# Reordering the front of a fused attention and SwiGLU block on one core: load order, rounding order, and where the attention units are placed

## The chip, the core and the metric

The kernel runs on one core of a Trainium2 chip. The metric is device time in microseconds (us) of one launch. The engines are named as in the profile: PE multiplies matrices, DVE works on vectors, ACT computes activations and copies, POOL (GpSimd) is a second vector engine that cannot read PSUM, and SP issues transfers. PE loads its weights ahead of its matmuls; this shows as PEld. Each engine works through its own queue in order and waits for the others by semaphores. Transfers issued by SP and ACT run on 16 shared DMA engines.

## The reference

The block takes 2048 rows of 448 numbers in float32. It normalises each row, computes attention of 16 heads of width 28 that share one key and one value projection, adds the result to the input, normalises again, and applies a SwiGLU block of width 1792 with a second residual.

```python
xn = layernorm(x)                       # no scale, no shift, eps 1e-5
q  = (xn @ wq) in 16 heads of 28;  k = xn @ wk;  v = xn @ wv   # wk, wv: 448 x 28
p  = softmax(q @ k.T * 28 ** -0.5)
h  = x + (p @ v, heads side by side) @ wo
y  = layernorm(h)
out = h + (silu(y @ w1) * (y @ w3)) @ w2
```

## The kernel before

The rows are cut into four quarters t of 512 (`X[t]`, four blocks n of 128 rows each). Products that need float32 precision are made of three matmuls with rounded operands (type float32r): an operand a is split into a rounded part and the remainder, and rounded times rounded, remainder times rounded, and rounded times remainder are summed in one PSUM bank. `mm_D` does this over the 448 inputs, which are three blocks of 128 and one of 64. The last block carries the rounded part in partitions 0 to 63 and the remainder in 64 to 127, so a full product is 3 x 3 + 2 = 11 matmuls. `mm_D` calls `between` after the sixth of them, so that other matmuls can stand inside a product.

The order of work is written out by hand (the pool is set to a manual schedule): each engine's queue has its instructions in the order in which the Python code makes them. There are eight PSUM banks; `bank()` hands out the one that was given back longest ago, and a matmul into it waits until the earlier user's readers are done.

**The front** is everything ahead of the main loop. It does the following.

- Loads. SP issues X[0] in four blocks, then WQ (line 408, three transfers), then X[1] to X[3] (line 410). ACT issues WK and WV (line 407, three transfers each: three full blocks, and the 64-row block twice). The transfers share eight semaphores, so a later transfer also waits until an earlier one on the same semaphore has landed.
- Weights. `split_wkv` (L429 to L431) copies WK to a second place and makes the rounded part of WK and WV on ACT and the remainder on POOL. `split_wq` (L441) rounds WQ in four steps on ACT; `low_wq` (L437) makes the four remainders on POOL.
- Layer norm of quarter t. `ln_stats` (L178, L179) on DVE; `ln_rstd` adds eps on DVE (L183) and takes the power -0.5 on POOL (L184); `ln_norm` (L189) subtracts the mean and multiplies by the inverse root on DVE, one block at a time, and a narrow copy on POOL (L191) repeats the last 64 columns. The loop calls it with `spare` for POOL.
- `tr(t)`: four times `ln_tr`. PE transposes four blocks (L203), ACT rounds the result into `xh` (L211), DVE takes the remainder into `xl` (L221; L223 for the last 64 columns). For t = 0 the transposes of the first column block are interleaved with `heat`, matmuls whose results are not used (L420).
- `kv(t)`: keys and values. ACT copies them out (L473, L475), SP copies the keys to partitions 64 to 127 (L476), and, for odd t, POOL subtracts the keys of the quarter before (L478, `KD`). `k_low(t)` takes the remainder of the keys on DVE (L483), SP copies it (L484), and the bank is given back. `va(t)` transposes the values (L490) and copies them (L491).
- `q(t, g)`: queries of four heads. ACT copies them out (L502); for the first it rounds them, and DVE takes the remainder (`build_qs`, L238, L239).
- `quads()`: the row maxima of the scores for the softmax, for two quarters of keys at a time. A unit is four heads by 128 queries by 512 keys. Its first half multiplies the queries with the key difference `KD`, and ACT takes the positive part (L257, L267); its second half multiplies with the keys of the first quarter, and DVE adds both and takes the maximum (L271). Each half takes four banks. The list `first` holds twenty halves in order, and one call of `quads()` issues the next one.

The part of the written order that the change touches stands in lines 516 to 563. The **main loop** then goes over 16 groups of four heads and 512 queries and 16 blocks of keys (lines 629 to 660): scores and exponentials (L308, L318), products with the values (L326), and the row maxima of the groups ahead (L257, L263). The feed-forward part follows (lines 749 to 773).

Of the kernel before, what the change touches and what calls it, by code (L numbers as in the profile page):

```python
# [8 lines left out]
F32 = mybir.dt.float32  # L9
F32R = mybir.dt.float32r  # L10
AF = mybir.ActivationFunctionType
ALU = mybir.AluOpType
# [4 lines left out]
P = 128  # L17
S = 2048
D = 448
H = 16  # L20
DH = 28
F = 1792
T = 512
NT = S // T
NQ = T // P
# [15 lines left out]
def block_kernel(  # L41
# [13 lines left out]
    ve, se, ge, pe, sy = nc.vector, nc.scalar, nc.gpsimd, nc.tensor, nc.sync  # L55
    xv = x[0].rearrange("(t p n) d -> t p n d", t=NT, p=P, n=NQ)
# [3 lines left out]
    def f(ap):  # L60
        return ap.bitcast(F32)
# [4 lines left out]
    ln_pool = ctx.enter_context(tc.tile_pool(name="ln", bufs=2))  # L66
# [5 lines left out]
    X = [keep.tile([P, NQ, D], F32, name=f"X{t}") for t in range(NT)]  # L72
    ident = keep.tile([P, P], F32, name="ident")
    NEG = [keep.tile([P, 32], F32R, name="neg")] * 2
    NGT = [keep.tile([P, 32], F32, name=f"ngt{k}") for k in range(2)]
    pexp = keep.tile([P, NQ], F32, name="pexp")
# [3 lines left out]
    def slot(k, dt, name):  # L80
        return slots.tile([P, 2, T], dt, name=name, tag=f"slot{k}")

    QSP, PTP, WSP, HIDP = [4, 0, 1], [9, 5, 6, 7, 8], [(0, 1), (2, 3), (4, 5)], [6, 7, 8, 9]
    KD = slot(2, F32R, "kd")
# [6 lines left out]
    KH = keep.tile([P, S], F32R, name="KH", tag="kh")  # L91
# [37 lines left out]
    def bank(name="pb"):  # L129
        k = free.pop(0)  # L130
        ps = ps_w.tile([P, T], F32, name=name, tag=f"bank{k}") if k < 7 else ps_o.tile([P, T], F32, name=name, tag="po")
        used[id(ps)] = ps, k
        return ps

    def done(ps):
        free.append(used.pop(id(ps))[1])
# [2 lines left out]

    def mm_D(ps, lhs, rhs, lsl, rsl, between=None, part=False):


        terms = []
        for a, b in ((0, 0), (1, 0), (0, 1)):
            terms += [(a, c, b, c) for c in range(3)]
        terms += [(0, 3, 0, 3), (0, 3, 1, 3)][: 2 - part]
        for k, (a, ca, b, cb) in enumerate(terms):
            pe.matmul(  # L150
                ps, lhs[b][:, cb, lsl], rhs[a][:, ca, rsl],
                start=(k == 0), stop=(k == len(terms) - 1 and not part),
            )
            if between is not None and k == 5:
                between()

    def load_w(dst, w, eng=sy):
        eng.dma_start(dst[:, 0:3], w[0:384].rearrange("(c p) m -> p c m", p=P))
        eng.dma_start(dst[0:64, 3], w[384:448])
        eng.dma_start(dst[64:128, 3], w[384:448])  # L160
# [9 lines left out]
    LN = {}  # L170

    def ln_stats(t, n):
        if n == 0:
            LN[t] = (ln_pool.tile([P, NQ, 6], F32, name="st", bufs=NT),
                     ln_pool.tile([P, NQ, 2], F32, name="mv", bufs=NT),
                     ln_pool.tile([P, NQ], F32, name="rs", bufs=NT), {})
        st, mv, _, _ = LN[t]
        ve.bn_stats(st[:, n], X[t][:, n])  # L178
        ve.bn_aggr(mv[:, n], st[:, n])  # L179

    def ln_rstd(t, n0=0, n1=NQ):
        _, mv, rs, _ = LN[t]
        ve.tensor_scalar(rs[:, n0:n1], mv[:, n0:n1, 1], EPS, None, op0=ALU.add)  # L183
        ge.tensor_tensor(rs[:, n0:n1], rs[:, n0:n1], pexp[:, n0:n1], op=ALU.pow)  # L184

    def ln_norm(t, n, spare=False):
        _, mv, rs, xns = LN[t]
        xn = xns[n] = ln_pool.tile([P, 512], F32, name="xn", bufs=4)
        (ge if spare else ve).tensor_scalar(xn[:, :D], X[t][:, n], mv[:, n, 0:1], rs[:, n : n + 1],  # L189
                                            op0=ALU.subtract, op1=ALU.mult)  # L190
        ge.tensor_copy(xn[:, D:], xn[:, 384:D])  # L191

    XT = {}
# [35 lines left out]
    def build_qs(i, ps=None, spare=False):  # L229
        t, g = divmod(i, NG)  # L230
        QS[i] = slot(QSP[i % 3], F32R, "qs")
        MX[i] = MXS[i % 2]
        qh, ql = QS[i][:, 0], QS[i][:, 1]
        q = QR[t][:, g] if ps is None else ps
        if spare:
            ge.tensor_copy(qh, q)
        else:
            se.activation(qh, q, AF.Copy)  # L238
        (ge if ps is None else ve).tensor_tensor(ql, q, f(qh), op=ALU.subtract)  # L239
# [159 lines left out]
    def wkv(tl, k):  # L399
        return tl[:, k, :384].rearrange("p (c m) -> p c m", c=4)  # L400

    RELU2, VT = slot(5, F32, "relu2"), slot(8, F32, "vt")
    wkv_r, WKV = wkv(slot(7, F32, "wkv"), 0), slot(6, F32R, "wkvs")
    WKV = [wkv(WKV, k) for k in range(2)]
    ve.memset(wkv_r, 0.0)
    for m0, w in ((0, wk), (64, wv)):
        load_w(wkv_r[:, :, m0 : m0 + DH], w, se)
    load_w(wq_r, wq)
    for t in range(1, NT):
        sy.dma_start(X[t], xv[t])  # L410
    kb = keep.tile([64, 1], F32, name="kb")
    ge.tensor_tensor(kb, ident[:64, 28:29], ident[:64, 60:61], op=ALU.add)
    for k in range(2):
        ve.memset(f(WQ[k][:, :, :, DH:]), 0.0)
    se.activation(NGT[0][:, :P // 4], ident[:, :P // 4], AF.Copy)
    warm = bank()

    def heat(n):
# [16 lines left out]
    def low_wq(c0, c1, eng):  # L435
        for c in range(c0, c1 + 1):
            eng.tensor_tensor(WQ[1][:, c, :, :DH], wq4[:, c], f(WQ[0][:, c, :, :DH]), op=ALU.subtract)  # L437

    def split_wq(c0, c1, eng=None):
        for c in range(c0, c1 + 1):  # L440
            se.activation(WQ[0][:, c, :, :DH], wq4[:, c], AF.Copy)  # L441
            if eng:
                low_wq(c, c, eng)

    def load_wo():
        ge.memset(wo_r, 0.0)
        wov = wo.rearrange("(g j r) e -> j r g e", j=4, r=DH)
        for j in range(4):
            sy.dma_start(wo_r[32 * j : 32 * j + DH], wov[j])
# [2 lines left out]
        ve.tensor_copy(WO[0][:, g], wo_r[:, g])  # L452
        ge.tensor_tensor(WO[1][:, g], wo_r[:, g], f(WO[0][:, g]), op=ALU.subtract)

    def stats(t, *ns):
        for n in ns:
            ln_stats(t, n)
        if NQ - 1 in ns:
            ln_rstd(t)

    def norm(t):
        for n in range(NQ):
            ln_norm(t, n)

    def tr(t, *cs):
        for c in cs or range(4):
            ln_tr(t, c)

    def kv(t, between=None):
        cols = slice(t * T, (t + 1) * T)  # L470
        ps = bank()
        mm_D(ps[:96], WKV, XT[t], slice(0, 96), slice(0, T), between)
        se.activation(KH[0:64, cols], ps[0:64], AF.Identity, bias=kb)  # L473
        vt = VT[:, t % 2]
        se.activation(vt[64:96], ps[64:96], AF.Copy)  # L475
        sy.dma_start(f(KH[64:128, cols]), f(KH[0:64, cols]))  # L476
        if t % 2:
            ge.tensor_tensor(KD[:, t // 2], f(KH[:, cols]), f(KH[:, (t - 1) * T : t * T]), op=ALU.subtract)  # L478
        return vt, ps

    def k_low(t, ps):
        cols = slice(t * T, (t + 1) * T)
        ve.scalar_tensor_tensor(KL[0:64, cols], ps[0:64], kb, f(KH[0:64, cols]), op0=ALU.add, op1=ALU.subtract)  # L483
        sy.dma_start(f(KL[64:128, cols]), f(KL[0:64, cols]))  # L484
        done(ps)

    def va(t, vt):
        ps = bank()
        for n in range(NQ):
            pe.transpose(ps[:, 32 * n : 32 * n + 32], vt[64:96, n * P : (n + 1) * P], ident[64:96, 64:96])  # L490
        ve.tensor_copy(VA[:, NQ * t : NQ * t + NQ, :DH],  # L491
                       ps[:, :P].rearrange("p (n r) -> p n r", n=NQ)[:, :, :DH])
        done(ps)

    def q(t, g, between=None):
        ps = bank()
        mm_D(ps, [w[:, :, 4 * g : 4 * g + 4].rearrange("p c h r -> p c (h r)") for w in WQ],
             XT[t], slice(0, P), slice(0, T), between)
        if t == g == 0:
            build_qs(0, ps)  # L500
        else:
            se.activation(QR[t][:, g], ps, AF.Copy)  # L502
        done(ps)
# [6 lines left out]
    def quads(n=1):  # L510
        while n > 0 and first:
            fn, *args = first.pop(0)
            fn(*args)
            n -= fn is quad

    for n in range(NQ):
        ln_stats(0, n)
        ln_rstd(0, n, n + 1)
        if n > 0:
            ln_norm(0, n - 1)  # L520
    ln_norm(0, NQ - 1)
    split_wkv()
    split_wq(0, 3)
    ln_tr(0, 0, between=lambda: heat(8))
    done(warm)
    tr(0, 1, 2, 3)
    low_wq(0, 3, ge)
    v0, p0 = kv(0)
    stats(1, 0, 1, 2, 3)
    q(0, 0)  # L530
    k_low(0, p0)
    norm(1)
    q(0, 1)
    tr(1)
    v1, p1 = kv(1)
    stats(2, 0, 1, 2, 3)
    q(0, 2)
    k_low(1, p1)
    norm(2)
    q(0, 3)  # L540
    va(0, v0)
    va(1, v1)
    build_qs(1)
    quads()
    tr(2)
    quads()
    v2, p2 = kv(2, quads)
    stats(3, 0, 1, 2, 3)
    q(1, 0, quads)
    k_low(2, p2)  # L550
    norm(3)
    quads()
    q(1, 1, quads)
    va(2, v2)
    quads()
    q(1, 2, quads)
    q(1, 3)
    build_qs(2)
    quads()
    tr(3)  # L560
    quads()
    v3, p3 = kv(3)
    load_wo()
    q(2, 0)
    k_low(3, p3)
# [14 lines left out]
    def at(s, fn, *args):  # L580
        todo.setdefault(s, []).append((fn, args))
# [8 lines left out]
    LAST = NC * NI  # L590
# [9 lines left out]
            at(e + 14 + 2 * n, ln_stats, t, n)  # L600
        at(e + 22, ln_rstd, t)
    for n in range(NQ):
        at(LAST - 24 + n, ln_norm, 0, n, True)
    for c in range(4):
        at(LAST - 17.5 + 4 * c, lambda c: ln_tr(0, c, True, True), c)
    for t in range(NT):
# [195 lines left out]
```

## Time and profile before

| | |
|---|---|
| median of three runs | 1195.46 us (1195.0 to 1196.61) |
| profiled execution, its own time | 1196.01 us |
| its span, first to last instruction | 1194.2 us |
| mean granted PE clock | 0.998 |
| PE busy | 1178.6 us, 99% |
| DVE, ACT, POOL busy | 811.2, 724.0, 332.4 us |
| first matmuls of the main loop | 92.75 us after the span's start |

The profile is read by rows. In an answer in order of time a row is: start, length in us, engine, line, operation, what is written and read, shapes, how many instructions were merged, and, in brackets, the idle time before and what ended it. `PEq`, `ACTq`, `SPq` are an engine's queue: issuing of a transfer, or waiting. A matmul's length includes its way through the array; successive matmuls start closer together than that. In a row of a group, the numbers behind the bar are the total busy time in us, the mean length of one in ns, and the idle time ahead of them with what ended it.

### The profile page before, as it was taken

What the parts mean: (1) busy time and instruction counts of PE and PEld (TensorE: products, weight loads), DVE (VectorE), ACT (ScalarE), POOL (GpSimd) and SP (SyncE); (2) the same over time, 40 slices, a digit from 0 to 9 for tenths busy, and PEclk for the clock granted to TensorE, in tenths of its full rate; (3) what the DMA queues carried; (4) which work ended last, traced back from release to release, by engine and by line L of the source; (5) the groups of instructions that cost most, each with busy time, mean ns of one, the idle gap of its engine ahead of it and who ended that gap; (6) DMA issues with size and microseconds to landing.
All of it is one profiled execution on the core that took longest, in us unless ns stands there. A gap on an engine that the chain in (4) does not pass through costs nothing. (4 is left out here: it accounts for less than half of the span.)

```text
span 1194.2 us, 24111 instructions
## 1 busy us (share of the span) xinstructions
PE 1178.6 (99%) x9594; PEld 728.6 (61%) x9594; DVE 811.2 (68%) x1486; ACT 724.0 (61%) x1377; POOL 332.4 (28%) x256
## 2 busy tenths in 40 slices
PE   8999999999999999999999999999999999999998
PEld 6664444445544445444445443688888888888886
DVE  6758999998899997899997982254444445444333
ACT  3568999997799996899996999411211111111111
POOL 4211011101101110110110132363555455445552
PEclk9999999999999999999999999999999999999999
DMA  5010001000001000010000010114000000000000
GB/s 167 19 37 2 27 10 46 11 12 2 11 4 44 12 12 2 11 47 5 8 12 10 2 46 11 40 45 117 1 32 1 1 1 31 1 1 32 1 1 32
DMA packets 32377, 26.92 MB, mean 23 GB/s; under 512 B 10824, under 2 KB 28936, under 8 KB 32264
## 3 DMA queue, kind: packets, MB, share of 16 engines
q1 hardware_dynamic: 31144, 25.27, 7.2%
q8 instruction: 75, 1.23, 0.4%
q14 instruction: 38, 0.31, 0.1%
q10 hardware_dynamic: 1120, 0.12, 0.1%
HBM read 20.25 MB, written 3.80 MB: 20 GB/s over the span
## 5 line engine op out<-in xcount | busy, mean ns | idle before, releaser
L318 ACT ACTIVATE pt<-pb 128x512 f32<-128x512 f32 x1024 | 531.5, 613 | 11.5 <-PE pb L308 5.5
L263 DVE TENSOR_REDUCE mx<-pa 128x1 f32<-128x512 f32 x708 | 460.7, 684 | 53.4 <-PE pb L308 38.1
L308 PE MATMUL pb<-qs,KH 32*128 32x512 f32 x2048 | 343.1, 431 | 0.1
L257 PE MATMUL pa<-KH,qs 32*128 32x512 f32 x866 | 326.6, 487 | 0.0
L326 PE MATMUL po<-pt,VA 128*32 128x256 f32 (+1 forms) x2984 | 298.2, 471 | 5.6 <-ACT OT L330 5.2
L308 PE MATMUL pb<-qs,KL 32*128 32x512 f32 x1024 | 284.6, 419 | 0.0
L308 PEld LDWEIGHTS pb<-qs,KH 32*128 32x128 f32 x2048 | 174.9, 183 | 113.9 <-DVE mx L263 50.1
L150 PE MATMUL pa<-xh,w 128*128 128x512 f32 x784 | 202.2, 391 | 0.0
L694 ACT ACTIVATE rb<-pa 128x512 f32<-128x512 f32 x56 | 30.4, 596 | 251.9 <-PE pa L686 251.9
L150 PEld LDWEIGHTS pa<-xh,w 128*128 128x128 f32 x784 | 146.2, 188 | 30.3 <-issue 1.2
L257 PEld LDWEIGHTS pa<-KH,qs 32*128 32x128 f32 x866 | 142.5, 182 | 9.5 <-issue 2.2
L711 PE MATMUL pb<-w2s,hid 128*128 128x448 f32 x672 | 145.0, 371 | 0.8 <-POOL w2s L380 0.8
L308 PEld LDWEIGHTS pb<-qs,KL 32*128 32x128 f32 x1024 | 136.6, 182 | 2.4
L711 PEld LDWEIGHTS pb<-w2s,hid 128*128 128x128 f32 x672 | 123.9, 188 | 21.5 <-issue 10.0
L326 PEld LDWEIGHTS po<-pt,VA 128*32 128x32 f32 x2984 | 59.1, 108 | 122.6 <-issue 105.3
L267 ACT ACTIVATE relu<-pa 128x512 f32<-128x512 f32 x158 | 91.7, 600 | 54.9 <-PE pa L257 38.6
L271 DVE CUSTOM_DVE_ANT_0 relu<-pa,relu 128x512 f32<-128x512 f32 x158 | 105.5, 682 | 11.3 <-ACT relu L267 9.7
L372 POOL TENSOR_TENSOR w<-QR,w 128x1024 fp32r<-128x1024 f32 x32 | 83.9, 2636 | 95.0 <-PE pa L686 81.4
L703 DVE TENSOR_TENSOR hid<-rb,hid 128x512 fp32r<-128x512 f32 x56 | 72.1, 1287 | 39.2 <-ACT hid L702 39.2
L350 POOL TENSOR_TENSOR OT<-OT,rb 128x512 f32<-128x512 f32 x16 | 20.5, 1283 | 273.9 <-ACT pt L318 102.8
L150 PE MATMUL pa<-xl,w 128*128 128x512 f32 x336 | 94.5, 390 | 0.0
L371 DVE CAST w<-QR 128x1024 fp32r<-128x1024 f32 x32 | 22.2, 694 | 90.5 <-PE pa L150 82.3
(96 smaller groups left out, 955.5 us busy)
## 6 DMA issues: line engine op xcount, KB each, us to landing
rb<-sd SPq DMA_DIRECT2D x64, 64.0 KB
QR<-in_B_w_dram SPq DMA_DIRECT2D x16, 192.0 KB
X<-in_A_x_dram SPq DMA_DIRECT2D x3, 896.0 KB
out_dram<-X SPq DMA_DIRECT2D x3, 896.0 KB
w<-in_B_w_dram SPq DMA_DIRECT2D x8, 192.0 KB
w_wo<-in_B_w_dram SPq DMA_DIRECT2D x6, 224.0 KB
qs<-ngt SPq DMA_DIRECT2D x64, 2.0 KB
sm<-OT SPq DMA_DIRECT2D x64, 2.0 KB
```

Source lines behind the costliest of these rows:

```text
L150: pe.matmul(ps, lhs[b][:, cb, lsl], rhs[a][:, ca, rsl], start=(k == 0), stop=(k == len(terms) - 1 and not part),)
L257: pe.matmul(self.ps, QS[i][r, 0, n * P : (n + 1) * P], ks[r], start=True, stop=True)
L263: ve.tensor_reduce(self.col(), self.ps, axis=AX.X, op=ALU.max)
L267: se.activation(r, self.ps, AF.Relu)
L271: ve.tensor_tensor_reduce(r, self.ps, r, 1.0, LOW, op0=ALU.add, op1=ALU.max, accum_out=self.col())
L308: pe.matmul(self.ps, (KH, KH, KL)[k][r, c * P : (c + 1) * P], QS[i][r, (0, 1, 0)[k]], start=(k == 0), stop=(k == 2))
L318: se.activation(pt, self.ps, AF.Exp, bias=0.0, scale=SCALE)
L326: pe.matmul(PO[i][32 * j : 32 * j + 32, q], VA[:, c], PT[i, c, j][:, q], start=(c == 0 and h0 == 0), stop=(c == NC - 1 and h1 == 2))
L372: ge.tensor_tensor(wl, W13[k], f(wh), op=ALU.subtract)
L694: se.activation(sg, ps[0], AF.Silu)
L703: ve.tensor_tensor(h[:, 1], sg, f(h[:, 0]), op=ALU.subtract)
L711: pe.matmul(Y[t][n][:, :D], hid[a][:, n * P : (n + 1) * P], w2s[:, b, :D], start=(k == 0 and m == 0), stop=(k == NF - 1 and m == 2))
```

## The change

- WV is loaded by SP, behind X[0], and no longer by ACT; X[1] is loaded next, ahead of WQ; X[2] and X[3] follow WQ. WK stays on ACT's queue.
- The small fill of `NGT[0]` on ACT reads the constant `pexp` and stands ahead of WQ's issue in the order.
- `split_wq(0, 3)` moves behind `tr(0, 1, 2, 3)`: ACT rounds the transposed x before it rounds WQ.
- In `q`, the product of the rounded 64-column block comes ahead of the three products with WQ's remainders (`lows_last`).
- `k_low(0)` and `norm(1)` move ahead of `q(0, 0)`; `k_low(1)` ahead of `q(0, 2)`.
- The subtraction of the keys leaves `kv` and becomes `k_diff(t)`. For t = 1 it stands behind `stats(2)`, whose inverse root is on the same engine (POOL).
- `norm(3)` runs on ACT, as `Identity` with scale and bias. The bias, minus mean times inverse root, is made by two more POOL operations on 128 x 4 (`nbias`). `norm(2)` moves behind `q(0, 2)` as it did, with `k_low(1)` ahead.
- The unit halves stand at other places: `q(1, 0)` and two halves now come ahead of `tr(2)`, one half moves from behind `tr(2)` and one from behind `tr(3)` to between the projections. Their order and number are the same.

```diff
+        if lows_last:
+            terms.insert(6, terms.pop(9))
...
+        if nbias:
+            ge.tensor_tensor(nb, mv[:, :, 0], rs, op=ALU.mult)
+            ge.tensor_scalar(nb, nb, -1.0, None, op0=ALU.mult)
...
+        if eng is se:
+            se.activation(xn[:, :D], X[t][:, n], AF.Identity, bias=nb[:, n : n + 1], scale=rs[:, n : n + 1])
+        else:
+            eng.tensor_scalar(xn[:, :D], X[t][:, n], mv[:, n, 0:1], rs[:, n : n + 1],
+                              op0=ALU.subtract, op1=ALU.mult)
...
-        load_w(wkv_r[:, :, m0 : m0 + DH], w, se)
+        load_w(wkv_r[:, :, m0 : m0 + DH], w, sy if m0 else se)
+    se.activation(NGT[0], pexp[:, :1].to_broadcast([P, 32]), AF.Copy)
+    sy.dma_start(X[1], xv[1])
     load_w(wq_r, wq)
-    for t in range(1, NT):
+    for t in range(2, NT):
         sy.dma_start(X[t], xv[t])
...
-    se.activation(NGT[0][:, :P // 4], ident[:, :P // 4], AF.Copy)
...
-        if t % 2:
-            ge.tensor_tensor(KD[:, t // 2], f(KH[:, cols]), f(KH[:, (t - 1) * T : t * T]), op=ALU.subtract)
         return vt, ps
+
+    def k_diff(t):
+        ge.tensor_tensor(KD[:, t // 2], f(KH[:, t * T : (t + 1) * T]), f(KH[:, (t - 1) * T : t * T]),
+                         op=ALU.subtract)
...
     split_wkv()
-    split_wq(0, 3)
     ln_tr(0, 0, between=lambda: heat(8))
     done(warm)
     tr(0, 1, 2, 3)
+    split_wq(0, 3)
     low_wq(0, 3, ge)
     v0, p0 = kv(0)
-    stats(1, 0, 1, 2, 3)
+    stats(1)
+    k_low(0, p0)
+    norm(1, ve)
     q(0, 0)
-    k_low(0, p0)
-    norm(1)
     q(0, 1)
     tr(1)
     v1, p1 = kv(1)
-    stats(2, 0, 1, 2, 3)
+    stats(2)
+    k_diff(1)
+    k_low(1, p1)
     q(0, 2)
-    k_low(1, p1)
-    norm(2)
+    norm(2, ve)
     q(0, 3)
     va(0, v0)
     va(1, v1)
     build_qs(1)
     quads()
+    q(1, 0, quads)
+    quads()
     tr(2)
-    quads()
     v2, p2 = kv(2, quads)
-    stats(3, 0, 1, 2, 3)
-    q(1, 0, quads)
-    k_low(2, p2)
-    norm(3)
+    stats(3, True)
     quads()
     q(1, 1, quads)
+    norm(3, se)
+    k_low(2, p2)
     va(2, v2)
     quads()
     q(1, 2, quads)
+    quads()
     q(1, 3)
     build_qs(2)
     quads()
     tr(3)
-    quads()
     v3, p3 = kv(3)
+    k_diff(3)
```

More of the change, by code (lines that the diff above doesn't have):

```diff
@@ L136, in done, with mm_D @@
         free.append(used.pop(id(ps))[1])
-    def mm_D(ps, lhs, rhs, lsl, rsl, between=None, part=False):
+    def mm_D(ps, lhs, rhs, lsl, rsl, between=None, part=False, lows_last=False):
         terms = []
@@ L175, in ln_stats, with ln_rstd, ln_norm @@
                      ln_pool.tile([P, NQ, 2], F32, name="mv", bufs=NT),
-                     ln_pool.tile([P, NQ], F32, name="rs", bufs=NT), {})
-        st, mv, _, _ = LN[t]
+                     ln_pool.tile([P, NQ], F32, name="rs", bufs=NT), {},
+                     ln_pool.tile([P, NQ], F32, name="nb", bufs=NT))
+        st, mv = LN[t][:2]
         ve.bn_stats(st[:, n], X[t][:, n])
         ve.bn_aggr(mv[:, n], st[:, n])
-    def ln_rstd(t, n0=0, n1=NQ):
-        _, mv, rs, _ = LN[t]
+    def ln_rstd(t, n0=0, n1=NQ, nbias=False):
+        _, mv, rs, _, nb = LN[t]
         ve.tensor_scalar(rs[:, n0:n1], mv[:, n0:n1, 1], EPS, None, op0=ALU.add)
         ge.tensor_tensor(rs[:, n0:n1], rs[:, n0:n1], pexp[:, n0:n1], op=ALU.pow)
-    def ln_norm(t, n, spare=False):
-        _, mv, rs, xns = LN[t]
-        xn = xns[n] = ln_pool.tile([P, 512], F32, name="xn", bufs=4)
-        (ge if spare else ve).tensor_scalar(xn[:, :D], X[t][:, n], mv[:, n, 0:1], rs[:, n : n + 1],
-                                            op0=ALU.subtract, op1=ALU.mult)
+        if nbias:
+            ge.tensor_tensor(nb, mv[:, :, 0], rs, op=ALU.mult)
+            ge.tensor_scalar(nb, nb, -1.0, None, op0=ALU.mult)
+    def ln_norm(t, n, eng=ve):
+        _, mv, rs, xns, nb = LN[t]
+        xn = xns[n] = ln_pool.tile([P, 512], F32, name="xn", bufs=4)
+        if eng is se:
[3 more added lines that the diff above has]
+                              op0=ALU.subtract, op1=ALU.mult)
         ge.tensor_copy(xn[:, D:], xn[:, 384:D])
@@ L453, in split_wo, with stats, norm @@
         ge.tensor_tensor(WO[1][:, g], wo_r[:, g], f(WO[0][:, g]), op=ALU.subtract)
-    def stats(t, *ns):
-        for n in ns:
+    def stats(t, nbias=False):
+        for n in range(NQ):
             ln_stats(t, n)
-        if NQ - 1 in ns:
-            ln_rstd(t)
-    def norm(t):
+        ln_rstd(t, nbias=nbias)
+    def norm(t, eng):
         for n in range(NQ):
-            ln_norm(t, n)
+            ln_norm(t, n, eng)
     def tr(t, *cs):
@@ L497, in q @@
         mm_D(ps, [w[:, :, 4 * g : 4 * g + 4].rearrange("p c h r -> p c (h r)") for w in WQ],
-             XT[t], slice(0, P), slice(0, T), between)
+             XT[t], slice(0, P), slice(0, T), between, lows_last=True)
         if t == g == 0:
@@ L602, in block_kernel @@
     for n in range(NQ):
-        at(LAST - 24 + n, ln_norm, 0, n, True)
+        at(LAST - 24 + n, ln_norm, 0, n, ge)
     for c in range(4):
```

## The prediction

> **What bounds the kernel now.** I read the page first, then the stretches of the front by window, then its queues in order of time.
>
> ```profile
> span 1194.2 us, 24111 instructions
> ...
> PE 1178.6 (99%) x9594; PEld 728.6 (61%) x9594; DVE 811.2 (68%) x1486; ACT 724.0 (61%) x1377; POOL 332.4 (28%) x256
> ```
>
> ```profile
> 6.10:9.80 3.70, 3.54 (x32) 3.18 (x30) 2.78 (x9) 0.91 (x3) 2.39 (x7) 1.00 1.04 282
> 10.00:16.00 6.00, 4.73 (x21) 2.81 (x20) 3.51 (x7) 3.82 (x8) 5.22 (x5) 0.89 1.01 409
> 11.25:14.66 3.41, 2.21 (x7) 0.98 (x8) 2.24 (x4) 2.57 (x6) 3.41 (x4) 1.00 1.02 420
> 14.66:18.07 3.41, 3.41 (x10) 2.42 (x9) 3.23 (x9) 0.99 (x2) 0.56 (x1) 0.50 0.51 209
> 33.48:65.28 31.80, 29.87 (x151) 18.75 (x151) 23.57 (x64) 19.74 (x37) 6.81 (x12) 1.00 0.04 9
> 65.28:92.75 27.47, 27.47 (x134) 17.72 (x133) 15.78 (x50) 15.25 (x29) 2.82 (x2) 1.00 0.17 40
> ```
>
> Columns: window, length, busy PE, weight load, DVE, ACT, POOL, granted clock, DMA share, GB/s. PE is busy 99% of the span, and every edit lies ahead of q(2,0), at 65.28. From there to the main loop (92.75) PE has no idle time, so I take a shift of q(2,0) to reach the end unchanged. Only three stretches can give: up to tr(1) at 22.66 (with 3.41 us at half clock), tr(1) with kv(1), and 33.48 to 65.28.
>
> **Stage A, up to tr(1): the order of loads, of ACT, and DVE's k_low.**
>
> ```profile
> 5.06 0.39 SPq L158 DMA_DIRECT2D OT<-in_A_wq_dram  x1
> 6.73 1.54 SPq L410 DMA_DIRECT2D X<-in_A_x_dram  x3
> 9.59 1.58 PE L203 MATMUL pb<-ident,xn 128*128 128x128 f32 x13
> 9.90 1.98 ACT L441 ACTIVATE OS<-OT 128x448 fp32r<-128x448 f32 x4 [2.78 <-DMA OT<-in_A_wq_dram]
> 10.77 4.45 POOL L437 TENSOR_TENSOR OS<-OT,OS 128x448 fp32r<-128x448 f32 x4
> 11.79 2.04 ACT L211 ACTIVATE xh<-pb 128x512 fp32r<-128x512 f32 x4
> 12.39 1.89 DVE L221 TENSOR_TENSOR xl<-pb,xh 128x512 fp32r<-128x512 f32 x3 [2.94 <-ACT xh L211]
> 12.41 1.45 PE L150 MATMUL pb<-xh,wkvs 128*96 128x512 f32 x3 [1.24 <-ACT xh L211]
> 14.31 0.69 DVE L223 TENSOR_TENSOR xh<-pb,xh 64x512 fp32r<-64x512 f32 x1
> 16.75 1.47 PE L150 MATMUL pb<-xh,OS 128*128 128x512 f32 x3
> 18.34 1.02 POOL L184 TENSOR_TENSOR rs<-rs,pexp 128x4 f32<-128x4 f32 x1 [3.12 <-DVE rs L183]
> 22.02 1.76 DVE L189 TENSOR_SCALAR xn<-X,mv,rs 128x448 f32<-128x448 f32 x4
> 22.66 2.82 PE L203 MATMUL pb<-ident,xn 128*128 128x128 f32 x16
> ```
>
> ACT serves WQ (9.90) before the rounded x, although PE has c0 transposed by about 9.9. With x first, xh starts at 9.95 instead of 11.79, or 1.84 earlier. In before, L223 ends 3.2 after xh's start; now at 13.16. PE's transposes end at 11.17, so kv(0) runs from 11.15, waits a little for xl, and gives PE free at about 13.9 (11 matmuls at 0.233 us, the pitch of eight in 2.03 at 29.65, below) instead of 16.75. It also fills the window 11.25 to 14.66, which held only 7 matmuls and was followed by 0.50 clock.
>
> WQ pays. Issued at 5.06, it was ready at 9.88. WV on SP is three more issues ahead of it, and the third I take to wait for WK's first transfer, as WQ's first did (the SP wait below), so that X[1] goes out at about 5.7. X[1] is 0.92 MB, 2.24 us at 409 GB/s. WQ itself moved at 282 GB/s in a start that X[1] now takes over. Bounds: ready at 11.85, where ACT is free of xh anyway, or 13.3 if X[1] adds all of its time and the later issues count too; I take 12.3, the sum less half of that start. WQ's rounding then has c0 at 12.95, and POOL's four low parts (4.45 for four) end at 17.45. q(0,0) from 13.9 has nine matmuls done by 16.4 and waits for the last low part; moving the term of the rounded last block ahead of the lows spends one matmul of that wait and cannot shorten it, as the last term needs the fourth low part. Its last matmul is at 17.5, q(0,1)'s at 20.06, tr(1) starts at **20.3**, instead of 22.66. Stats of X[1] start at 13.16 (0.92 MB ahead of WQ lands by 10.5), the inverse root follows the low parts on POOL at 17.45 to 18.47, and norm(1), no longer behind q(0,0)'s DVE subtraction, is done by 20.3. **Gain 2.4**; 2.8 at best, 1.4 at worst.
>
> WV off ACT's queue, its table load at 3 instead of 4.78, and a fill source that is ready earlier cost and give nothing: WKV was rounded by 7.1 and is not used before 11. KL(0) on SP goes earlier and waits for nobody there.
>
> **Stage B, tr(1) and kv(1).**
>
> ```profile
> SPq L158 <- DMA wkv<-in_A_wk_dram: 2.5, 1, 2.5
> ```
>
> ```profile
> 24.20 2.06 ACT L211 ACTIVATE xh<-pb 128x512 fp32r<-128x512 f32 x4 [0.92 <-PE pb L203]
> 28.25 0.86 PE L150 MATMUL pb<-xh,OS 128*128 128x512 f32 x3
> 29.65 2.03 PE L150 MATMUL pb<-xh,OS 128*128 128x512 f32 x8
> 30.54 0.17 DVE L183 TENSOR_SCALAR rs<-mv 128x4 f32<-128x4 f32 x1
> 31.51 1.29 POOL L478 TENSOR_TENSOR kd<-KH 128x512 fp32r<-128x512 f32 x1 [7.27 <-DMA KH<-KH]
> 32.76 1.02 POOL L184 TENSOR_TENSOR rs<-rs,pexp 128x4 f32<-128x4 f32 x1
> 33.48 0.49 PE L490 MATMUL pb<-ident,vt 32*128 32x32 f32 x5
> ```
>
> norm(1) at 22.02 fed tr(1) one block per 0.42 us, so xh came 1.54 after tr(1) began. With all blocks ready it is 0.7 after: 21.0. From xh to q(0,2) it was 28.25 − 24.20 = 4.05, so q(0,2) starts at 25.05 and va, 5.23 later as before, at **30.25** against 33.48. **Gain 0.85 more, 3.25 in all.**
>
> k_diff behind the inverse root: stats(2) ended at 30.71, 2.46 after q(0,2)'s start, so now at 27.5; the root runs to 28.55, norm(2) from there on DVE. The difference started 3.26 after q(0,2), when its copy of KH had landed (28.3 now), so it runs from 28.55 to 29.85 if undisturbed; the four narrow copies of xn behind it have until tr(2). The first unit needs it 0.28 after va, at 30.53. KL(1)'s place on SP and DVE's k_low(1) keep their order; k_diff(3) stays ahead of WO's fill on POOL. But norm(2) runs beside it:
>
> ```profile
> 22.65 0.81 POOL L191 COPY xn<-xn 128x64 f32<-128x64 f32 x1 [3.29 <-DVE xn L189]
> ...
> 9.52 0.24 POOL L191 COPY xn<-xn 128x64 f32<-128x64 f32 x1 [0.42 <-DVE xn L189]
> ```
>
> Beside norm(1) a copy of 0.24 took 0.81. At the rate of two copies (0.48) in 1.14 us, the difference ends at 30.9: **0.3 lost**. Bounds: nothing, or all of norm's 1.76, ending at 31.65 (1.1 lost). The Trainium skill (SBUF — State Buffer, Who interferes with whom) says that a VectorE tensor_scalar in a two-port mode and a GpSimd op exclude each other for the whole instruction, whoever issues first going ahead; by it the loss would be 0 or 1.1.
>
> **Stage C, from va to q(2,0), 31.80.** The units are the same, 40 matmuls ahead of kv(3); only their places move, and norm(3) goes to ACT.
>
> ```profile
> 36.51 2.10 ACT L211 ACTIVATE xh<-pb 128x512 fp32r<-128x512 f32 x4
> 40.57 0.49 PE L257 MATMUL pa<-kd,qs 32*128 32x512 f32 x1 [0.23 <-DVE mx L271]
> 62.61 0.94 PE L150 MATMUL pb<-xh,wkvs 128*96 128x512 f32 x3 [0.73 <-DVE xl L221]
> ...
> L271 DVE CUSTOM_DVE_ANT_0 relu<-pa,relu 128x512 f32<-128x512 f32 x18 | 11.4, 684 | 1.6 <-PE pa L257 1.5
> L267 ACT ACTIVATE relu<-pa 128x512 f32<-128x512 f32 x20 | 10.9, 602 | 2.1 <-DVE mx L271 2.0
> L189 DVE TENSOR_SCALAR xn<-X,mv,rs 128x448 f32<-128x448 f32 x8 | 3.5, 504 | 2.3 <-POOL rs L184 2.3
> ```
>
> I walk each queue from 30.25 with these rows (four relus 2.05 at their pitch, four maxima 2.45, four xh 2.10, xl with L223 2.6, half a unit between matmuls 0.64). First relus 31.4 to 33.4, first maxima 33.0 to 35.45. The second relus follow q(1,0)'s copy, 34.8 to 36.85, and hold xh(2) behind them: kv(2) starts at 37.45, although tr(2) ends at 36.5 (0.9 idle). Second maxima 40.1 to 42.55, stats(3) to 45.8, third maxima to 48.25. The root on POOL and two 4-wide products end at 47.3, and norm(3) on ACT runs to 49.2 (four at 0.48, from xh). Behind it wait the fourth relus, 49.2 to 51.25, where ACT was free at 46.3; PE meanwhile waits for banks to 48.35. q(1,3) ends at 54.4, the last maxima run from 55.2 to 57.65 and hold xl(3), so kv(3), ready at 56.9, ends at 60.65 and q(2,0) starts at 60.9. That is 30.65 for the stage: **gain 1.15**, less the 0.3. Bounds: 26.1 if PE never waited (six projections of 2.56, two transposes of 1.95, ten halves of 0.64, 0.5 for va), and 32.8, one more than now, if ACT, off DVE by 1.76 us of norm, becomes the bound. A walk like this misses waits, so I keep 30.65.
>
> **The sum** is 2.4 + 0.85 − 0.3 + 1.15 = 4.1 us off the profiled execution's 1196.0 (span 1194.2), thus 1191.9; off the runs' median, 1195.46, it is **1191.4**.
>
> **Rivals.** (1) The half-clock stretch stays. For: WQ late leaves PE waiting in q(0,0), 1.1 of the 3.41 after 14.66, and a threshold isn't in the trace. Against: 7 matmuls brought it on, 11 to 14 now stand there. Price: ten matmuls at half pace, up to 1.7; 1.5 gives 1192.9. The Trainium skill (TensorE: Matmul & The Clock Gate, What's actually happening) has half rate come back after at least one idle window of about 3.4 us. By it 1.24 us of idle was not the cause and filling it removes nothing; the trace, with half clock behind a window of 7 matmuls, leans the other way. (2) ACT becomes the bound of stage C: relus behind norm(3) cost a further 2 us, the stage takes 32.6, leaving 2.2: 1193.3. Against: ACT was busy 19.74 of 31.80. (3) Slower: WQ decides. If X[1] and the waits in SP's order hold it back past 14.7, tr(1) is no earlier than 22.66, PE idles over 2 us, and the half-clock stretch moves onto q(0,1) and tr(1). At 16.5 that is 1.8 late plus 1.7, less stages B and C (1.7): 1197.3; the loss begins at 14.7. Against: 409 GB/s with larger packets. (4) It doesn't do what it says: the loop waits for something unmoved and the gain is lost ahead of it, 1195.5. Against: no PE idle from 65.28 on.
>
> **How the numbers follow.** Forecast 0.62, (1) 0.15, (2) 0.13, (3) 0.05, (4) 0.05. The forecast's own range is 1189.6 to 1192.9, from the bounds of WQ (−0.4, +1.0), of the difference (−0.3, +0.8) and a like error of the walk; with (1) and (2) it is **1189.3 to 1194.3**. 0.2%, about what a measurement here tells from no change, is 2.4 us: faster needs under 1193.07. That is the forecast, most of (1) and a third of (2): 0.80. Same takes the rest of these and (4): 0.16; slower 0.04.
>
> **What would show it.** kv(0)'s first matmul near 11.2; WQ's rounding near 12.3; no half clock in 11 to 18; tr(1) near 20.3; va near 30.25, its first unit by 30.9; q(2,0) near 61.2; the loop near 88.7. Wrong would be a WQ past 14, half clock behind it, or relus queued behind norm(3) past 50.

## The result and the profile after

The changed kernel takes **1199.32 us** (median; 1198.29 to 1200.91) against 1195.46 (1195.0 to 1196.67): ratio 1.0031, 95% interval 1.002 to 1.0042. It is slower by 3.9 us, where 1191.4 was forecast, range 1189.3 to 1194.3.

The page of the changed kernel:

```profile
span 1197.6 us, 24122 instructions
...
PE 1182.7 (99%) x9594; PEld 727.8 (61%) x9594; DVE 812.1 (68%) x1482; ACT 726.3 (61%) x1381; POOL 332.7 (28%) x258
```

The front in order of time, rows of ACT, POOL, DVE and PE:

```profile
9.98 2.07 ACT L220 ACTIVATE xh<-pb 128x512 fp32r<-128x512 f32 x4 [2.52 <-PE pb L212]
12.48 1.98 ACT L451 ACTIVATE OS<-OT 128x448 fp32r<-128x448 f32 x4 [0.43 <-DMA OT<-in_A_wq_dram]
13.14 4.49 POOL L447 TENSOR_TENSOR OS<-OT,OS 128x448 fp32r<-128x448 f32 x4 [2.28 <-ACT OS L451]
20.58 1.91 PE L212 MATMUL pb<-ident,xn 128*128 128x128 f32 x16
28.84 1.30 POOL L489 TENSOR_TENSOR kd<-KH 128x512 fp32r<-128x512 f32 x1
28.91 2.74 DVE L198 TENSOR_SCALAR xn<-X,mv,rs 128x448 f32<-128x448 f32 x4 [0.36 <-POOL rs L187]
30.53 0.49 PE L501 MATMUL pb<-ident,vt 32*128 32x32 f32 x5
48.31 2.71 ACT L196 ACTIVATE xn<-X,nb,rs 128x448 f32<-128x448 f32 x4 [1.11 <-POOL nb L190]
50.93 2.03 ACT L276 ACTIVATE relu<-pa 128x512 f32<-128x512 f32 x4
63.68 0.86 PE L152 MATMUL pb<-xh,OS 128*128 128x512 f32 x3
```

And by window (window, length, busy PE, weight load, DVE, ACT, POOL, granted clock, DMA share, GB/s):

```profile
45.63:49.05 3.42, 2.88 (x13) 1.27 (x11) 3.35 (x13) 1.35 (x4) 1.45 (x3) 1.00 0.00 0
49.05:52.46 3.41, 3.35 (x10) 2.11 (x10) 0.84 (x3) 3.41 (x8) 0.95 (x4) 0.50 0.17 41
30.53:63.68 33.15, 31.00 (x152) 18.73 (x151) 22.97 (x64) 21.81 (x41) 6.32 (x13) 0.95 0.04 9
63.68:91.09 27.41, 27.41 (x135) 17.70 (x133) 14.11 (x44) 15.25 (x29) 2.83 (x2) 1.00 0.18 40
755.10:1197.60 442.50, 437.93 (x2000) 356.37 (x1999) 194.69 (x273) 77.29 (x130) 215.10 (x125) 1.00 0.07 22
```

The part of the kernel before that answers to the last row begins at 757.58, with the last copy of the attention output:

```profile
757.58:1194.20 436.62, 431.68 (x2000) 355.90 (x1999) 193.14 (x273) 77.22 (x130) 214.55 (x125) 1.00 0.07 23
```

The account, changed against before: the changed kernel starts tr(1) 2.08 us earlier (20.58, 22.66), va 2.95 earlier (30.53, 33.48), q(2,0) 1.60 earlier (63.68, 65.28) and the loop 1.66 earlier (91.09, 92.75), and it ends attention 2.48 earlier. Then the feed-forward part, in which no line of the order was touched, takes **442.5 instead of 436.6 us**, and the gain becomes a loss of 3.4 (spans 1197.6 and 1194.2). So there were two questions: what slows the feed-forward part, and where the gain of stage C (from va to q(2,0)) went.

In order of time, a stretch of the feed-forward part of the kernel before:

```profile
869.87 1.75 PE L150 MATMUL pa<-xh,w 128*128 128x512 f32 x7
871.46 0.84 PE L150 MATMUL pa<-xl,w 128*128 128x512 f32 x3
```

and of the changed kernel:

```profile
871.16 1.79 PE L152 MATMUL pa<-xh,w 128*128 128x512 f32 x7
872.78 0.85 PE L152 MATMUL pa<-xl,w 128*128 128x512 f32 x3
```

From the start of the first row to the start of the second, seven matmuls take 1.59 us before and 1.62 after. The pitch is the time from the start of one matmul to the start of the next of its kind. Its mean over the part (steps up to 250 ns, worked out from all starts in the trace) goes from 227.2 to 232.4 ns for the products of xh and xl with the weights w, and from 204.4 to 205.1 for those of hid with w2s. PE waits for nobody in either stretch. 1120 products (784 with xh, 336 with xl) x 5.2 ns and 672 x 0.7 make 6.3 us; measured 5.9.

What differs there is the place of the tiles. The new `nb` tiles, four of 16 bytes in each partition, each on 32, lie between `rs` and `xn`, and so xn, sm, rb and all ten slots (w and hid among them) lie 128 bytes further on; xh, xl and w2s lie where they did. The rival was the order in which PSUM banks are handed out, which the new order of the front may leave different when the loop begins.

### The profile page after: what moved, and what is told of

Same layout as the page of the kernel before. It is cut to its first block, busy times and chain, and to the rows that moved or that the text cites. A ratio compares the mean times of both kernels' runs of the same rounds, so it can differ in the third digit from the quotient of the medians.

```text
span 1197.6 us, 24122 instructions
## 1 busy us (share of the span) xinstructions
PE 1182.7 (99%) x9594; PEld 727.8 (61%) x9594; DVE 812.1 (68%) x1482; ACT 726.3 (61%) x1381; POOL 332.7 (28%) x258
## 5 line engine op out<-in xcount | busy, mean ns | idle before, releaser
L152 PE MATMUL pa<-xh,w 128*128 128x512 f32 x784 | 205.9, 396 | 0.0
L707 ACT ACTIVATE rb<-pa 128x512 f32<-128x512 f32 x56 | 30.5, 596 | 257.5 <-PE pa L699 257.5
```

The source lines that it names most:

```text
L152: pe.matmul(ps, lhs[b][:, cb, lsl], rhs[a][:, ca, rsl], start=(k == 0), stop=(k == len(terms) - 1 and not part),)
L707: se.activation(sg, ps[0], AF.Silu)
```

## Experiments on the place of the tiles

**1. nb behind the slots, all else as changed.**

```diff
+    nb_pool = ctx.enter_context(tc.tile_pool(name="nbs", bufs=2))     # after slots
-                     ln_pool.tile([P, NQ], F32, name="nb", bufs=NT))
+                     nb_pool.tile([P, NQ], F32, name="nb", bufs=NT))
```

> The changed kernel, with the four new nb tiles placed behind all other tiles, so that xn, sm, rb and the ten slots lie where they lay in the kernel before (in the changed kernel they lie 128 bytes further on in each partition). Theory P (the shift of these tiles makes each of the feed-forward matmuls on xh and xl wait about 5 ns longer, 227 to 232 ns, some 6.2 us over the part from 757 us on): the pitch is back at 227 ns and the time falls to 1193.1. Rival B (the other order in which PSUM banks are handed out when the main loop begins is what slows them): nothing changes, 1199.3 and 232 ns.

1193.66 us, ratio to before 0.9989 (0.9979 to 0.9999); pitches 227.2 and 204.4 ns. Its window of the feed-forward part:

```profile
755.13:1191.60 436.47, 431.65 (x2000) 355.59 (x1999) 193.50 (x273) 77.24 (x130) 215.04 (x125) 1.00 0.07 23
```

The 442.5 us of the part are 436.5 again. 5.7 us of the time (1199.32 less 1193.66) hang on where 128 bytes are put.

**2. The kernel before with 128, 64, 256 and 192 unused bytes ahead of xn.** (n = 32, 16, 64 and 48 numbers of 4 bytes.)

```diff
+            if t == 0:
+                ln_pool.tile([P, n], F32, name="pad", bufs=1)
```

> The kernel before, with an unused 128-byte tile ahead of xn, so that its tiles lie exactly as in the changed kernel; the order of work and of the banks is that of before. Theory P: the feed-forward matmuls on xh and xl are 232 ns apart and the time is 1201.7 (6.2 more). Rival B: 227 ns and 1195.5.

> The kernel before, with 64 bytes unused ahead of xn. Theory P, if what counts is the place of the slots within 256 bytes against xh and xl: an intermediate or an equal pitch, 227 to 232 ns, 1195.5 to 1201.7; it only tells which places are good. Rival B: 1195.5.

> The kernel before, with 256 bytes unused ahead of xn. Theory P with a period of 256 bytes: 227 ns and 1195.5, as without; with a longer period 232 ns and about 1201. Rival B: 1195.5.

> The kernel before, with 192 bytes unused ahead of xn, so that the slots with w and hid start at a multiple of 256 bytes. Theory P says only that the pitches are set by this place: for xh and xl with w 227 ns at 64, 233 at 128, 232 at 192 so far; for hid with w2s 204, 201, 205. At 0 I have no forecast of the sign: 222 to 233 and 200 to 206, 1189 to 1201. Rival B (banks): 227 and 204, 1195.

128 bytes: 1199.62 (ratio 1.0038, 1.0023 to 1.0053), pitches 232.4 and 205.1, the numbers of the changed kernel, with the order and the banks of before. 64 bytes: 1200.49 (1.0041, 1.0026 to 1.0056), 233.2 and 201.2. 256 bytes: 1195.42 (1.0001, 0.9991 to 1.001), 227.1 and 204.4, as without. 192 bytes, a single run: 1195.56, 228.9 and 201.5. The forecast of 1201.7 for 128 was 2 us too high; the profiled execution has no half clock in the front, but whether that is the reason is not shown. For 64, the pitch of 233.2 lies above the 227 to 232 that were expected. The banks are out as a cause; the place of the slots decides, with a period of 256 bytes as far as these four points tell. The window of the feed-forward part with 128 bytes shows it by itself:

```profile
754.88:1197.30 442.42, 437.78 (x2000) 356.38 (x1999) 194.37 (x273) 77.31 (x130) 214.75 (x125) 1.00 0.07 22
```

**3. xh, xl and the slots shifted together by 128 bytes, kernel before.**

```diff
+            if t == 0:
+                xt_pool.tile([P, 32], F32, name="pad", bufs=1)
```

> The kernel before, with 128 bytes unused ahead of xh, so that xh, xl and the slots with w all lie 128 bytes further: the place of w against xh is that of before, its own place within 256 bytes is that of the changed kernel. Theory R (what counts is w's place against the xh and xl that stream beside it): 227 ns for xh and xl with w, about 1195.7 with hid's pitch at 205. Rival W (w's own place counts): 232 ns and 1200.

1195.25 (0.9998, 0.9989 to 1.0008), 227.3 ns for xh and xl with w, 205.3 for hid with w2s, which did not move along. So it is the place of w against the xh and xl that stream beside it, and not w's own place: with w moved against them by 0, 64, 128 and 192 bytes, counted from the kernel before, the pitch is 227.2, 233.2, 232.4 and 228.9. Why the distance matters no row shows.

**4. hid alone 64 bytes further** (on the kernel of experiment 1).

```diff
+    for k in range(6):
+        slots.tile([P, 2, T], F32, name=f"s{k}", tag=f"slot{k}")
+    slots.tile([P, 16], F32, name="gap")
```

> The changed kernel with nb behind the slots, and 64 bytes unused ahead of the four slots that hold hid, so that hid lies 64 bytes further within 256 and the feed-forward weights w stay. Theory P (the place within 256 bytes sets the pitch of each product by itself): xh and xl with w stay at 227 ns, hid with w2s goes from 204.4 to about 201.2 as with 64 unused bytes ahead of everything; 672 x 3.2 ns = 2.2 us less, 1191.5. Rival (it is the place against other tiles, not of hid, that gave 201.2): 204.4 and 1193.7.

1191.77 (0.9969, 0.9958 to 0.9981), pitches 227.3 and 200.0: each of the two products can be given the best of the places tried without the other losing its own. The group of hid with w2s between 900 and 1100 us, first in the kernel before, then here:

```profile
L711 PE MATMUL pb<-w2s,hid 128*128 128x448 f32 x312 | 67.3, 371 | 0.0
```

```profile
L728 PE MATMUL pb<-w2s,hid 128*128 128x448 f32 x312 | 65.9, 367 | 0.0
```

## Experiments on the front

**5. The loads and the order of x and WQ alone, in the kernel before.**

```diff
-        load_w(wkv_r[:, :, m0 : m0 + DH], w, se)
+        load_w(wkv_r[:, :, m0 : m0 + DH], w, sy if m0 else se)
+    sy.dma_start(X[1], xv[1])
     load_w(wq_r, wq)
-    for t in range(1, NT):
+    for t in range(2, NT):
...
-    split_wq(0, 3)
     ln_tr(0, 0, between=lambda: heat(8))
     done(warm)
     tr(0, 1, 2, 3)
+    split_wq(0, 3)
```

> The kernel before with the loads reordered (WV by SP, X[1] ahead of WQ) and x rounded ahead of WQ, nothing else. Theory H (these parts only keep PE from the idle time that brings half clock; POOL's remainders of WQ end no earlier than before): tr(1) starts at 20.3 to 20.7, as the kernel before with 128 unused bytes had it in an undisturbed profile (20.67), or later as norm(1) still waits for q(0,0); the time is 1194 to 1195. Theory of the prediction (a gain of 2.4 by itself): 1192.8.

1194.03 (0.9991, 0.9982 to 1.0000); tr(1) at 20.73. The gain in time is 0.9, with an interval that reaches none, and not 2.4. The old order, in the execution with 128 unused bytes, had no half clock and this:

```profile
9.46 1.98 ACT L443 ACTIVATE OS<-OT 128x448 fp32r<-128x448 f32 x4 [2.10 <-DMA OT<-in_A_wq_dram]
...
20.67 2.81 PE L205 MATMUL pb<-ident,xn 128*128 128x128 f32 x16
```

That is 11.21 from WQ's rounding to tr(1). With 64 and 192 unused bytes and in experiment 3 the two stand at 10.69 and 21.90, 10.63 and 21.82, 10.57 and 21.78: 11.2 each. In the profile that I forecast from they stand at 9.90 and 22.66, or 12.76 apart, as 3.41 us at half clock lay between; with 256 unused bytes, again with half clock between, they are 12.62 apart. So in the old order tr(1) hangs on when WQ lands. In the changed kernel WQ's rounding comes at 12.48, 8.1 ahead of tr(1) at 20.58. Against the four executions of the old order named here without half clock that is 0.1 to 1.3 us earlier; where the half clock falls between, about 1.5 more.

**6. Filling the idle time, kernel before.**

```diff
-    done(warm)
     tr(0, 1, 2, 3)
+    heat(11)
+    done(warm)
```

> The kernel before with eleven unused 128-column matmuls (0.11 us each) behind tr(0), in the 1.24 us in which PE waits for x. Theory I (PE's idle time between 11.2 and 14.7 brings the stretch of half clock): no half clock near 14.7, the loop starts at about 90.7 instead of 92.75, and the runs gather near 1193.8 instead of 1195.2. Rival (the stretch comes by the phase of the clock's windows whatever PE does there): as before, 1195.2.

1195.24 (0.9999, 0.999 to 1.0008), the loop at 92.67: the time that theory I forecast did not come, though its profile has no half clock in the front. WQ's rounding came at 11.39 in it, the latest of all, and tr(1) 11.21 later, at 22.60. So the run does not tell what brings the half clock. Idle time of PE is not enough to explain it. 3.41 us at half clock stood behind a window of the same length with only 7 matmuls in the kernel before, and behind one with 13 in the changed kernel (the row at 45.63 above). But with 192 unused bytes a window of this length with 7 matmuls, in which PE was idle for 1.1 us, was followed by full clock:

```profile
12.03:15.44 3.41, 2.29 (x7) 1.05 (x8) 2.31 (x4) 2.50 (x6) 3.41 (x4) 1.00 0.99 410
15.44:18.86 3.42, 3.42 (x17) 2.63 (x16) 3.22 (x10) 1.27 (x2) 0.77 (x1) 1.00 0.22 75
```

The stretches at half clock begin at another time in each execution (14.66, 14.73, 48.79, 49.05, 50.19), and the changed kernel with nb moved (experiment 1), same order, had none in the front. What decides it stays open.

**7. norm(3) on DVE, behind the half in q(1,2)** (on experiment 1).

```diff
-    stats(3, True)
+    stats(3)
...
-    norm(3, se)
...
     q(1, 2, quads)
+    norm(3, ve)
```

> The changed kernel with nb behind the slots (1193.66 us; va at 30.49, q(2,0) at 63.01), but norm(3) on DVE, behind the first half that stands in q(1,2), where DVE has 3.1 us idle. Theory N (stage C lost what was forecast because the fourth relus wait on ACT behind norm(3), which waits for two products on POOL and takes 2.72): the fourth relus start near 47.2 instead of 50.9, the stage from va to q(2,0) falls from 32.5 to about 30.8, the time by 1.7 to 1192.0. Rival D (DVE bounds the stage, and norm back on DVE costs it 1.76): stage 32.5 or longer, 1193.7 or more.

1194.08 (0.999, 0.9981 to 0.9999; experiment 1 had 0.9989) and 33.16 for the stage: the gain that theory N forecast did not come. The fourth relus did start at 46.78. PE still waited for banks, which the third maxima on DVE give back, and these stand behind stats(3) (rows of the queues of DVE, PE and ACT):

```profile
45.03 0.59 DVE L182 BATCH_NORM_STATS2 st<-X 128x6 f32<-128x448 f32 x1
...
45.99 0.69 DVE L281 CUSTOM_DVE_ANT_0 relu<-pa,relu 128x512 f32<-128x512 f32 x1
...
46.75 1.72 PE L267 MATMUL pa<-kd,qs 32*128 32x512 f32 x3 [0.29 <-DVE mx L281]
...
46.78 2.43 ACT L277 ACTIVATE relu<-pa 128x512 f32<-128x512 f32 x4
```

```profile
45.38:48.79 3.41, 2.77 (x12) 1.26 (x11) 3.34 (x12) 2.56 (x5) 1.01 (x1) 1.00 0.00 0
48.79:52.20 3.41, 3.41 (x11) 1.92 (x11) 0.57 (x2) 0.43 (x1) 0.00 (x0) 0.50 0.17 38
```

DVE is busy for 3.34 of the first 3.41 us, and half clock follows. Experiment 1's profile has no half clock in the stage, so 33.16 and its 32.52 cannot be compared as they stand. Half of the 3.41 us, 1.7, is an estimate of the most that the half clock cost here; without it the stage might have been as short as 31.5, and norm(3)'s place worth up to 1.0. The medians show nothing of that. That DVE's order holds the stage, by stats(3) ahead of the third maxima, is so far a reading of rows; experiments 8 and 9 test it.

**8. Another order for stage C** (on experiment 4).

```diff
     build_qs(1)
+    ln_stats(3, 0)
+    ln_stats(3, 1)
     quads()
     q(1, 0, quads)
+    ln_stats(3, 2)
+    ln_stats(3, 3)
+    ln_rstd(3)
     quads()
     tr(2)
     v2, p2 = kv(2, quads)
-    stats(3, True)
     quads()
     q(1, 1, quads)
-    norm(3, se)
     k_low(2, p2)
     va(2, v2)
     quads()
     q(1, 2, quads)
+    norm(3, ve)
     quads()
     q(1, 3)
     build_qs(2)
-    quads()
     tr(3)
-    v3, p3 = kv(3)
+    v3, p3 = kv(3, quads)
```

> The kernel with hid 64 bytes further (1191.77 us), with stage C put in another order: stats(3) in two pairs in DVE's idle time, ahead of the first maxima and ahead of xl(2), instead of ahead of the third maxima; norm(3) on DVE behind the half in q(1,2); the last half inside kv(3) instead of ahead of tr(3). Theory S (stage C was bound by DVE's order: stats(3) holds the third maxima and with them four banks, the last maxima hold xl(3)): va to q(2,0) takes 28.5 to 29.5 instead of 32.5, PE never works under half of a 3.4 us window, no half clock there, 1188.3. Rival D (DVE's amount of work bounds it, wherever it stands): 32 or more, 1191.8.

**1187.74** (1187.48 to 1188.02), ratio 0.9931 (0.9919 to 0.9944): less than both the kernel before and the changed one. The stage, first in experiment 1, then here, and two of the moved stats:

```profile
30.49:63.01 32.52, 29.96 (x151) 18.05 (x151) 22.98 (x64) 21.82 (x41) 6.34 (x13) 1.00 0.04 9
```

```profile
30.22:59.44 29.22, 28.37 (x151) 17.55 (x151) 23.42 (x63) 19.11 (x37) 6.30 (x11) 1.00 0.04 10
```

```profile
31.61 0.61 DVE L185 BATCH_NORM_STATS2 st<-X 128x6 f32<-128x448 f32 x1
...
35.84 0.62 DVE L185 BATCH_NORM_STATS2 st<-X 128x6 f32<-128x448 f32 x1
```

29.22 against 32.52, with DVE busy for no less (23.42 us; 22.98 there): its amount of work was not the bound of 32.52.

**9. The same with stats(3) back between kv(2) and the next half.**

> The same, but stats(3) stays where the changed kernel has it, between kv(2) and the next half; norm(3) and the last half stand as in the run beside it. Theory S: the third maxima again wait for the 3.2 us of stats(3); the stage takes 30.5 to 31.5, 1190.3. Rival (it is the last half ahead of xl(3) alone that cost the stage): as the run beside it, 1188.3.

1190.38 (0.9953, 0.9939 to 0.9966), as theory S had it: 2.6 us for the place of stats(3) alone. The profiled execution took 32.43 for the stage, above the forecast 30.5 to 31.5, and has the half clock at 50.19:

```profile
50.19:53.60 3.41, 3.41 (x11) 1.79 (x10) 1.83 (x5) 0.00 (x0) 0.00 (x0) 0.50 0.17 38
```

So the 2.6 may hold some half clock, which experiment 8's profile does not have: the five runs here lie between 1189.45 and 1191.4, those of experiment 8 within 0.6. Less an estimated 1.7, half of the 3.41, the stage would still be 1.5 longer than 29.22. What norm(3) on DVE and the last half inside kv(3) are worth, which lie between experiments 4 and 9 (ratios 0.9969 and 0.9953), no run tells apart.

## Why the prediction was wrong, step by step

- **The step that failed is in its first part: "every edit lies ahead of q(2,0) ... so I take a shift of q(2,0) to reach the end unchanged".** That held for the order: the loop began 1.66 earlier and attention ended 2.48 earlier. It did not hold for the memory. `nbias` brings a tile, the tile moves the slots by 128 bytes, and the feed-forward part, over 650 us later, takes 5.9 us more. None of the rivals had it; rival (4) had a lost gain, not a new cost. Experiments 1 and 2 show it from both sides. Of the 7.9 us between 1191.4 and 1199.32, 5.7 go when nb lies elsewhere; the other 2.3 are terms of the front, stages A and C below.
- **Stage A** was right in its times: WQ's rounding at 12.48 (12.3), the last low part at 17.6 (17.45), tr(1) at 20.58 (20.3), no half clock there. The size of the gain, 2.4, was not: it was taken against one execution, in which about 1.5 us were half clock that most other executions of the same order don't have. The loads and the order of x and WQ alone gave 0.9 in the median (experiment 5).
- **Stage B** was right: from tr(1) to va it takes 9.95 in the changed kernel and 10.82 in experiment 5, where norm(1) still waits; 0.85 forecast.
- **The key difference** cost nothing, not 0.3. It started at 28.84 and took 1.30, undisturbed, and the first unit came 0.28 after va, as before. norm(2), 0.07 later, took 2.74 instead of 1.76, all of it in its first block (1.47 instead of 0.50). The Trainium skill (SBUF — State Buffer, Who interferes with whom) has such a pair exclude each other, whoever issues first going ahead, and the trace agrees: DVE paid 0.98, with 1.7 us to spare ahead of the first maxima.
- **Stage C** was forecast at 30.65; it took 33.15, and 32.52 in experiment 1 without half clock, so that a gain of 1.15 became a loss. Two terms on ACT were mis-sized: norm(3) started at 48.31 instead of 47.3, and it took 2.71 instead of 1.9 (0.66 from one block to the next, 0.48 assumed). So the relus behind it came at 50.93 rather than 49.2, past the 50 that the prediction had named as a sign of being wrong. In experiment 1 the excess of 1.9 is 0.5 until PE has its banks and 1.4 over q(1,2) and q(1,3), where PE waits for these relus. Experiment 7 took norm(3) away from ACT, and the time stayed; whether half clock hid a gain there is open. What the walk took as given was DVE's order: stats(3) ahead of the third maxima, with PE waiting for banks to 48.35 (to 49.1 in the changed kernel). That this place of stats(3) costs time is shown by experiments 8 and 9. The stage came out at rival (2)'s price of 32.6, but its mechanism, ACT as the bound, was not what the runs bear out; that the figure agrees is luck. The last maxima ahead of xl(3) were seen, and priced as part of 30.65.
- **Half clock**: rival (1) looked for it in q(0,0). It came in stage C, behind the wait for banks. The rule that the prediction set beside it from the Trainium skill (TensorE: Matmul & The Clock Gate, What's actually happening), half rate after at least one idle window of about 3.4 us, is not what the rows show: PE was granted half clock behind stretches with 7 and 13 matmuls. Nor is the lean of the prediction, that 7 matmuls bring it on, borne out: full clock followed another window with 7 (experiment 6). The cause is open.

Left open: the 0.8 us that the loop gained by itself (1.66 at its start, 2.48 at the end of attention); what in the chip ties a matmul's pitch to the distance of its two operands; what brings the half clock.

## What to carry to other kernels

Compare where tiles lie as well as the order of work: a tile of a few bytes moves everything behind it, and here 128 bytes cost 5.9 us in a part that the change does not touch. Where an engine is full for a stretch, ask first in which order it gives back what others wait for (here banks, held by stats ahead of maxima), before moving work to another engine. Make the sum against several executions: what only some of them have, like the half clock ahead of tr(1) here, is not to be counted in full as a gain of the edit.

## What the runs showed of the hardware

- The pitch of back-to-back float32r matmuls, 512 columns with new weights each, depends on the distance between weights and moving operand: it is 227.2, 233.2, 232.4 and 228.9 ns as the weights move by 0, 64, 128 and 192 bytes from their place in the kernel before, and 227.1 at 256. For hid with w2s, 448 columns, it is 204.4, 200.0 to 201.2, 205.1 to 205.3 and 201.5 as hid moves by 64 bytes each time against w2s, and 204.4 at 256.
- An ACT activation of 448 columns with a scale and a bias for each partition came every 0.66 us, a plain copy of 512 columns every 0.5.
- WQ's landing varied: its rounding began at 9.46 to 11.39 us in kernels with the same loads in the same order, and tr(1) followed it by 11.2, or by 12.6 to 12.8 where 3.41 us at half clock lay between.
